# Layer 1's weight conversions with one step on ScalarE, splits in halves, and a new order at the front and in layer 2

## The chip, the core and the metric

One NeuronCore of a Trainium2 chip runs the whole program in one launch. Five engines work from queues of their own, each in order: TensorE (matmuls, and the weight loads that go beside them), VectorE (DVE in the rows), ScalarE (ACT), GpSimd (POOL) and SyncE (SP, which here issues every DMA). They wait for one another by semaphores. The metric is the time of one execution on the device in microseconds, the median of three runs.

## The reference

Three layers follow one another on 4 batches of 576 tokens, 2304 in all, 512 values each.

- Attention by landmarks, 8 heads of 64: `A = softmax(q k_lm)`, `Bm = softmax(q_lm k_lm)`, `C = softmax(q_lm k)`, where `q_lm` and `k_lm` are means over 18 tokens (32 landmarks). `Z` is an approximate inverse of `Bm` after six steps `Z = 2 Z - Z Bm Z`. The result is `A Z C v`.
- Layer 1: `h = x w_in` (512 to 2048), `g = h * clip(h + 3, 0, 6) / 6`, then `g w_out` (2048 to 512).
- Layer 2: the same shapes with `g = P(h) / (Q(h) + 1e-6)`, `P` a cubic with coefficients `a`, `Q = 1 + |b0| |h| + |b1| h^2`.

The four weight matrices arrive in 64-bit floating point, and the chip works in 32 bits. The inputs are drawn at a large scale, so that single-pass matmuls would not be precise enough.

## The kernel before, in words

*Precision.* Each large matmul is done as three: both factors are split into a high half (a copy to the type fp32r) and a low half (the value less the high one), and high x high, high x low and low x high are summed in PSUM. `split` (L95 to L104) writes the high half on one engine (mostly ScalarE, L99) and the low one on another (mostly GpSimd, L104).

*Weights.* Each matrix comes in 8 pieces of 1024 values on each of 128 partitions, 32 pieces in all, listed in `convs`: the first 16 are layer 1's (`wi` from `w_in`, `w1` from `w_out`), the others layer 2's. A piece is loaded by `cv_load` as raw 64-bit words, two DMAs of 512 KB, the first four into slabs, the later ones into a pool of two buffers. `cv_bits` (L134 to L148) makes 32-bit values of it: ScalarE scales the high word's absolute value into the exponent range (L145), VectorE shifts that left by three (L146), ors in the top three bits of the low word (L147) and ors in the sign (L148). The first four pieces go through it in halves, which gives 8 times 512 values, the other 28 whole. A `w1` or layer 2 piece is then split by `cv_split`; layer 2's halves are written to DRAM and come back when layer 2 begins. A `wi` piece is not split: it is stored, and loaded again for batches 1 to 3.

*The front of layer 1.* `w_in` is folded into attention: for each batch `T` (from `tmat`, a 64 x 32 matrix for each head) is multiplied with `w_in`, which gives `U` (`u_visit`, matmuls in L232, high half by ScalarE L495, low half by VectorE L496). Each quarter of `U` needs two `wi` pieces and serves four chunks. `AT` is the transposed `A`, made in two halves of a batch (`scores_a`, `soft_a1` to `soft_a3`).

*Chunks.* Layer 1 runs over 128 chunks: 8 blocks of 288 tokens by 16 chunks of 128 of the 2048 inner values. Blocks 0 and 1 take turns after 8 chunks, so that the later weights are wanted later. A chunk is `l1_in` (6 matmuls `psh`, L520; Relu on ScalarE, L523; `g` on VectorE, L525), `l1_split`, and four chunks later `l1_out` (12 matmuls into the four `psy` banks, L543). After a block's last chunk its `y` is evicted (L567 to L571) and stored.

*What sets the order.* Each step of attention, conversion and chunk is given a place by `at(place, f, ...)`; one unit is one chunk. The steps are emitted in the order of places, and a planner then orders the instructions of each engine by that priority and by a simulated timeline, in which an instruction that is ready may go ahead. The places are numbers in the table `PRM`: `f` and `a0`, `a1` for batch 0's attention, `cv` for conversions, `bt` for the attention of later batches, `u0`, `ul`, `uh` for batch 0's visits of `U`. Warm-up matmuls (`warm`) fill TensorE at the start.

*PSUM.* A pool `ps_l1` holds four banks shared by small results and `psh` (tag `psx`), and the four `psy` banks. When layer 1 is done, `ps_l2` is laid over them: four `ph` banks first, then `po`.

*Layer 2.* 48 units (6 blocks of 384 tokens by 8 pairs of inner chunks) in an order written out by hand: in turn n the matmuls `ph` of unit n (L730), its polynomial (`l2_poly`: ScalarE L740 and L741, `q` on GpSimd L742 and L743, or on VectorE in units listed in `FAST`), the split of unit n-1, the logarithm and exponential that stand for a division (L754, L755), the products on VectorE (L760 to L764), and the matmuls `po` of unit n-2 (L783). The units in `FAST` are worked in halves.

Of the kernel before, what the change touches and what calls it, by code (L numbers as in the profile page):

```python
# [36 lines left out]


PRM = dict(
    a0=[-53.53, -50.35, -44.44, -37.85],  # L40
    a1=[-28.73, -13.04, -13.56, -1.27],
    u0=-5.4,
    ul=2.4,
    uh=-0.88,
    nsl=4,
    f=[-78.2, -63.24, -60.85, -62.05, -59.74, -59.16, -58.38, -57.2, -56.3, -55.43, -55.23, -53.49, -53.31, -53.27, -52.82, -50.61, -43.53, -46.73, -41.98],
    fin=1.11,
    cv=[-62.23, -38.38, -34.15, -32.98, -29.24, -27.11, -6.27, -3.82, 6.49, 9.04, 10.58, 11.59, 12.99, 13.4, 14.91, 19.54],
    w0=32.18,
    ws=6.32,  # L50
    bt=[
# [11 lines left out]
def fused(ctx: ExitStack, tc: tile.TileContext, qT, kT, v, w_in, w_out, w2_in, w2_out, ca, cb, out):  # L63
# [26 lines left out]
    QC = 1.0 + 1e-6  # L90
    G.memset(lnb[:, 0:1], QC * 2.0 ** -LNS)
    G.memset(lnb[:, 1:2], -LNS * math.log(2.0))
    ca_s = const.tile([P, 4], F32, name="ca_s")
    cb_s = const.tile([P, 2], F32, name="cb_s")

    def split(dst_hi, dst_lo, src, hi_eng, lo_eng):

        if hi_eng is A:
            A.activation(dst_hi, src, AF.Copy)  # L99
        elif hi_eng is G:  # L100
            G.tensor_scalar(dst_hi, src, 1.0, 0.0, op0=ALU.mult, op1=ALU.add)
        else:
            V.tensor_copy(dst_hi, src)
        lo_eng.tensor_tensor(dst_lo, src, dst_hi.bitcast(F32), op=ALU.subtract)  # L104
# [26 lines left out]
            for h, t in enumerate(raw[key]):  # L131
                SP.dma_start(t.rearrange("p (a b) -> p a b", a=a // 2), src[:, h * a // 2:(h + 1) * a // 2])

    def cv_bits(key, h):  # L134
        if h == 0:
            val[key] = slab.tile([P, GW], F32, tag="slab", name="val")
        parts = raw[key]
        if h >= len(parts):
            return
        n = GW // len(parts)  # L140
        t = val[key][:, h * n:(h + 1) * n]
        i = t.bitcast(U32)
        w = parts[h].bitcast(U32).rearrange("p (n two) -> p n two", two=2)
        lo, hi = w[:, :, 0], w[:, :, 1]
        A.activation(t, hi.bitcast(F32), AF.Abs, scale=2.0 ** -112)  # L145
        V.tensor_scalar(i, i, 3, None, op0=ALU.logical_shift_left)  # L146
        V.scalar_tensor_tensor(i, in0=lo, scalar=29, in1=i, op0=ALU.logical_shift_right, op1=ALU.bitwise_or)  # L147
        V.scalar_tensor_tensor(i, in0=hi, scalar=0x80000000, in1=i, op0=ALU.bitwise_and, op1=ALU.bitwise_or)  # L148

    def cv_split(key):  # L150
        src = val.pop(key)
        hi = slab.tile([P, GW], F32R, tag="slab", name="whi")
        lo = slab.tile([P, GW], F32R, tag="slab", name="wlo")
        split(hi, lo, src, A, G)
# [41 lines left out]
    st = {}  # L196

    def psa(tag="psa"):
        return pp.tile([P, 512], F32, tag="psx" if tag in ("psa", "psh") else tag, name=tag, bufs=4 if tag in ("psa", "psh") else 1)

    def load_kq(b, cut=1):
        kx[b] = att.tile([P, NPAIR, S + LM], F32, tag="kx", name="kx")
# [323 lines left out]
    def l1_split(n):  # L528
        gg = hps.pop(n)
        t = w1p.tile([P, 2, HB], F32R, tag="ghl", name="ghl", bufs=5)  # L530
        split(t[:, 0, :], t[:, 1, :], gg, A, G)
        ghl[n] = t

    def l1_out(n):
        blk, c = turn[n]
        c0, c1 = (0, NFC - 1) if blk > 1 else (c - c % HC, c - c % HC + HC - 1)
        if c == c0:
            yps[blk] = [pp.tile([P, 512], F32, tag=f"psy{e}", name="psy") for e in range(NDC)]
        ps, t = yps[blk], ghl.pop(n)
# [76 lines left out]
    def at(place, f, *a):  # L616
        plan.append((place, len(plan), f, a))
# [39 lines left out]
        ):  # L657
            at(t, w, 0, h)
    for u in range(NG // 2):
        j = 2 * u  # L660
        at(PRM["u0"] if u == 0 else (2 * j if j < 4 else 2 * j + 8 - PRM["uh"]) - PRM["ul"], u_visit, 0, (u,))
    at(-100, warm, PRM["wm"][0], lambda: ident)
    at(f0[4] + 1e-3, warm, PRM["wm"][1], lambda: st[0, "qs"].rearrange("p a m -> p (a m)"))
    at(f0[6] + 1e-3, warm, PRM["wm"][2], lambda: st[0, "bd"][:, 0, 0].rearrange("p a m -> p (a m)"))
# [4 lines left out]
        cvp.append(PRM["cv"][i] if i < 2 * NG else PRM["w0"] + PRM["ws"] * (i - 2 * NG))  # L669
    for i in range(len(convs)):  # L670
        for h in range(2):
            at(cvp[i] + 0.1 * h, cv_bits, convs[i], h)
        at(cvp[i] + max(PRM["fin"], 0.2), cv3, convs[i])
        at(-99.5 + 0.1 * i if i < 4 else -98 + 0.01 * i if i < NSL else min(cvp[i - 2] + 0.9, cvp[i] - 0.1), cv0, i)

# [31 lines left out]
    l2_load = L2P["load"]  # L707
    pw1.__exit__(None, None, None)
    ps_l1.__exit__(None, None, None)


    l2p = L2P["p"]
# [84 lines left out]
                SP.dma_start(out[j * T2 + m * P:j * T2 + (m + 1) * P, :], o)  # L797

    NN = NB2 * NU2
    FAST = (0, 1, NN - 2, NN - 1)  # L800
    ms = tc.manual_schedule()
    ms.__enter__()
    for n in range(NN + 2):
        if n == 0:
            for j in range(NG):
                w2_load("i", j, (L2P["p"] if j == 0 else slab, slab))
                w2_load("o", j, (slab, slab))
        j, u = divmod(n, NU2)
# [75 lines left out]
```

## Time and profile before

| | us |
|---|---|
| median of 3 runs | 851.72 (850.27 to 851.88) |
| the profiled execution | 851.85 |
| its span, first to last instruction | 850.1 |
| TensorE busy | 818.7 (96%) |
| VectorE busy | 576.8 (68%) |
| ScalarE busy | 473.4 (56%) |
| GpSimd busy | 486.9 (57%) |
| mean granted clock of TensorE | 0.98 |

A busy share is a mean over stages. TensorE counts as busy while a matmul is under way, also at the lower clock and also for the warm-up matmuls, so its 96% say little of the front. The rows further down are of views that cut the execution by stage, by what an engine waited for, by kind of instruction and by order of time.

### The profile page before, as it was taken

What the parts mean: (1) busy time and instruction counts of PE and PEld (TensorE: products, weight loads), DVE (VectorE), ACT (ScalarE), POOL (GpSimd) and SP (SyncE); (2) the same over time, 40 slices, a digit from 0 to 9 for tenths busy, and PEclk for the clock granted to TensorE, in tenths of its full rate; (3) what the DMA queues carried; (4) which work ended last, traced back from release to release, by engine and by line L of the source; (5) the groups of instructions that cost most, each with busy time, mean ns of one, the idle gap of its engine ahead of it and who ended that gap; (6) DMA issues with size and microseconds to landing.
All of it is one profiled execution on the core that took longest, in us unless ns stands there. A gap on an engine that the chain in (4) does not pass through costs nothing.

```text
span 850.1 us, 14978 instructions
## 1 busy us (share of the span) xinstructions
PE 818.7 (96%) x5778; PEld 743.3 (87%) x5778; DVE 576.8 (68%) x935; ACT 473.4 (56%) x864; POOL 486.9 (57%) x353
## 2 busy tenths in 40 slices
PE   9769989999998999899999999999999999999998
PEld 8638879989898898889998889898989989898986
DVE  6989988695776646674228776665766675766666
ACT  3445665564564536655436656566656666565654
POOL 1249455553576325977315975766774775675551
PEclk9858999999999999999999999999999999999999
DMA  9765487393669205886891011011010010100101
GB/s 352 288 239 170 162 298 283 98 339 124 239 215 324 86 29 182 267 282 244 317 349 55 0 38 38 1 38 38 0 38 32 7 38 1 37 1 1 38 1 37
DMA packets 46312, 113.17 MB, mean 133 GB/s; under 512 B 6177, under 2 KB 14369, under 8 KB 45857
## 3 DMA queue, kind: packets, MB, share of 16 engines
q1 hardware_dynamic: 46240, 112.22, 37.6%
q8 instruction: 45, 0.74, 0.4%
q14 instruction: 27, 0.21, 0.1%
HBM read 81.79 MB, written 30.41 MB: 132 GB/s over the span
## 4 chain that ended last, share of the span: by engine, by line
PE 61%; DVE 15%; DMA 9%; ACT 5%; POOL 4%; issue 4%; SPq 0%; DVEq 0%; ACTq 0%; POOLq 0%
PE po L783 21%; PE ph L730 20%; PE psy L543 12%; PE psh L520 5%; DMA raw<-in_moe_w_in 3%; DMA qx<-in_q 3%; DVE val L148 3%; DVE val L147 2%; DMA yd<-y 2%; PE psa L232 1%; ACT val L145 1%; DVE val L146 1%; DVE g L525 1%; POOL ghl L104 1%; DMA wis<-wid 1%
## 5 line engine op out<-in xcount | busy, mean ns | idle before, releaser
L543 PE MATMUL psy<-ghl,whi 128*128 128x288 f32 x1024 | 217.8, 300 | 9.6 <-POOL ghl L104 5.2
L783 PE MATMUL po<-w2s,g2hl 128*128 128x512 f32 x864 | 210.4, 396 | 1.5 <-POOL g2hl L104 1.5
L730 PE MATMUL ph<-yhl,w2s 128*128 128x384 f32 x1152 | 208.5, 336 | 0.6 <-DVE y L571 0.6
L730 PEld LDWEIGHTS ph<-yhl,w2s 128*128 128x128 f32 x1152 | 202.1, 188 | 5.0 <-DVE y L571 0.8
L104 POOL TENSOR_TENSOR ghl<-g,ghl 128x288 fp32r<-128x288 f32 x128 | 135.0, 1064 | 120.2 <-ACT ghl L99 113.2
L783 PEld LDWEIGHTS po<-w2s,g2hl 128*128 128x128 f32 x864 | 161.8, 188 | 37.8 <-POOL g2hl L104 2.8
L543 PEld LDWEIGHTS psy<-ghl,whi 128*128 128x128 f32 x1024 | 167.7, 190 | 20.2 <-POOL ghl L104 6.7
L543 PE MATMUL psy<-ghl,wlo 128*128 128x288 f32 x512 | 149.1, 298 | 0.0
L520 PE MATMUL psh<-AT,us 128*128 128x288 f32 x768 | 127.8, 305 | 7.0 <-ACT us L495 3.4
L760 DVE SCALAR_TENSOR_TENSOR q<-q,r 128x768 f32<-128x768 f32 (+1 forms) x52 | 46.6, 895 | 114.7 <-ACT r L755 114.7
L520 PEld LDWEIGHTS psh<-AT,us 128*128 128x128 f32 x768 | 111.5, 194 | 11.1 <-ACT us L495 4.2
L742 POOL TENSOR_SCALAR q<-t,cb_s 128x768 f32<-128x768 f32 x44 | 56.0, 1272 | 102.1 <-ACT t L740 102.1
L104 POOL TENSOR_TENSOR g2hl<-g,g2hl 128x768 fp32r<-128x768 f32 (+1 forms) x52 | 89.8, 1729 | 34.1 <-ACT g2hl L99 34.1
L543 PEld LDWEIGHTS psy<-ghl,wlo 128*128 128x128 f32 x512 | 96.4, 189 | 1.2 <-issue 1.2
L525 DVE SCALAR_TENSOR_TENSOR g<-r,psh 128x288 f32<-128x288 f32 x128 | 56.8, 448 | 59.5 <-ACT r L523 42.7
L99 ACT ACTIVATE ghl<-g 128x288 fp32r<-128x288 f32 x128 | 55.7, 441 | 69.3 <-DVE g L525 62.5
L754 ACT ACTIVATE r<-q,lnb 128x768 f32<-128x768 f32 (+1 forms) x52 | 46.3, 890 | 81.4 <-POOL q L743 75.9
L743 POOL TENSOR_TENSOR q<-q,t 128x768 f32<-128x768 f32 x44 | 84.5, 1920 | 3.7
L523 ACT ACTIVATE r<-psh,three 128x288 f32<-128x288 f32 x128 | 62.7, 496 | 40.9 <-PE psh L520 40.9
L104 POOL TENSOR_TENSOR wlo<-val,whi 128x1024 fp32r<-128x1024 f32 x24 | 59.1, 2463 | 43.8 <-ACT whi L99 40.2
L740 ACT ACTIVATE t<-ph 128x384 f32<-128x384 f32 x96 | 47.0, 490 | 57.7 <-PE ph L730 57.3
L761 DVE SCALAR_TENSOR_TENSOR p<-p,ca_s,r 128x768 f32<-128x768 f32 (+1 forms) x52 | 64.6, 1243 | 0.0
(140 smaller groups left out, 995.2 us busy)
## 6 DMA issues: line engine op xcount, KB each, us to landing
raw<-in_moe_w_in SPq DMA_DIRECT2D x32, 512.0 KB, 5.7
raw<-in_moe_w_out SPq DMA_DIRECT2D x32, 512.0 KB, 5.7
wis<-wid SPq DMA_DIRECT2D x24, 512.0 KB, 7.1
w2s<-w2di SPq DMA_DIRECT2D x16, 512.0 KB, 6.2
w2s<-w2do SPq DMA_DIRECT2D x16, 512.0 KB, 5.8
yd<-y SPq DMA_DIRECT2D x32, 144.0 KB, 4.0
out<-o SPq DMA_DIRECT2D x18, 256.0 KB, 2.1
vx<-in_v SPq DMA_DIRECT2D x4, 1024.0 KB, 7.7
```

Of the source, the lines that this page charges most:

```text
L99: A.activation(dst_hi, src, AF.Copy)
L104: lo_eng.tensor_tensor(dst_lo, src, dst_hi.bitcast(F32), op=ALU.subtract)
L520: PE.matmul(ps[:, :HB], u[:, wp, f0:f0 + P], at[:, xp, g, :], start=(k == 0), stop=(k == 5))
L523: A.activation(r, ps[:, :HB], AF.Relu, bias=three)
L525: V.scalar_tensor_tensor(gg, in0=r, scalar=6.0, in1=ps[:, :HB], op0=ALU.min, op1=ALU.mult)
L543: PE.matmul(ps[e][:, :HB], w1[c // 2][wp][:, o + e * P:o + (e + 1) * P], t[:, xp, :], start=(c == c0 and i == 0), stop=(c == c1 and i == 2),)
L730: PE.matmul(ps[i][:, :T2], w2i[u][wp][:, d * 256 + i * P:d * 256 + (i + 1) * P], yh[:, xp, d, :], start=(k == 0), stop=(k == 11),)
L740: A.activation(t[:, i], h, AF.Abs)
L742: eng.tensor_scalar(q[:, cs], t[:, cs], cb_s[:, 1:2], cb_s[:, 0:1], op0=ALU.mult, op1=ALU.add)
L743: eng.tensor_tensor(q[:, cs], q[:, cs], t[:, cs], op=ALU.mult)
L761: V.scalar_tensor_tensor(p, in0=p, scalar=ca_s[:, 0:1], in1=r, op0=ALU.add, op1=ALU.mult)
L783: PE.matmul(ops[j][m], t[:, xp, i, m * P:(m + 1) * P], w2o[u][wp][:, i * DM:(i + 1) * DM], start=(c == 0 and k == 0), stop=(c == NFC - 1 a ...
```

## The change

`cv_bits` gets a flag. For all 16 pieces of layer 1 (`ka` lists 0 to 15) the shift by three is no instruction of its own: ScalarE reads the low word's top byte, divides it by 32, rounds down with a bias and writes the result as a 32-bit integer over the low word; VectorE then shifts and ors in one instruction. The bias is found at the start by two small instructions (`probe`) that tell how the conversion to an integer rounds. `cv_split` works in halves of 512, in both layers. In chunks from 96 on the low half of `g` is subtracted by VectorE instead of GpSimd. The `psx` banks get a pool of their own, opened ahead of `ps_l1`. In layer 2 unit 1 leaves `FAST`, and `q` is VectorE's in unit 0 only. Batch 0's four visits of `U` have places of their own (`ub`), and nearly all other places get new numbers.

```diff
-    a0=[-53.53, -50.35, -44.44, -37.85],
-    a1=[-28.73, -13.04, -13.56, -1.27],
-    u0=-5.4,
-    ul=2.4,
-    uh=-0.88,
+    a0=[-53.44, -49.77, -45.07, -40.67],
+    a1=[-29.09, -5.95, -16.01, -2.05],
+    ub=[-11.56, 2.59, 9.82, 14.37],
+    hc=8,
-    fin=1.11,
+    fin=0.75,
-    cv=[-62.23, -38.38, -34.15, -32.98, -29.24, -27.11, -6.27, -3.82, 6.49, 9.04, 10.58, 11.59, 12.99, 13.4, 14.91, 19.54],
-    w0=32.18,
+    cv=[-62.22, -38.38, -34.15, -33.16, -30.24, -27.99, -7.31, -4.94, 5.33, 7.88, 9.53, 12.36, 12.49, 13.12, 14.89, 21.57],
+    w0=31.92,
...
+    probe = const.tile([P, 3], F32, name="probe")
+    G.memset(probe[:, 0:1], 0.75)
+    A.activation(probe[:, 1:2].bitcast(I32), probe[:, 0:1], AF.Copy)
+    A.activation(probe[:, 2:3], probe[:, 1:2].bitcast(I32), AF.Copy, scale=-31.0 / 64.0)
+    floor_b = probe[:, 2:3]
...
         A.activation(t, hi.bitcast(F32), AF.Abs, scale=2.0 ** -112)
-        V.tensor_scalar(i, i, 3, None, op0=ALU.logical_shift_left)
-        V.scalar_tensor_tensor(i, in0=lo, scalar=29, in1=i, op0=ALU.logical_shift_right, op1=ALU.bitwise_or)
+        if by_act:
+            b = parts[h].bitcast(U8).rearrange("p (n k) -> p n k", k=8)[:, :, 3]
+            A.activation(lo.bitcast(I32), b, AF.Identity, bias=floor_b, scale=1.0 / 32.0)
+            V.scalar_tensor_tensor(i, in0=i, scalar=3, in1=lo, op0=ALU.logical_shift_left, op1=ALU.bitwise_or)
+        else:
+            V.tensor_scalar(i, i, 3, None, op0=ALU.logical_shift_left)
+            V.scalar_tensor_tensor(i, in0=lo, scalar=29, in1=i, op0=ALU.logical_shift_right, op1=ALU.bitwise_or)
         V.scalar_tensor_tensor(i, in0=hi, scalar=0x80000000, in1=i, op0=ALU.bitwise_and, op1=ALU.bitwise_or)
...
-        split(hi, lo, src, A, G)
+        for h in range(2):
+            c = slice(h * HW, (h + 1) * HW)
+            split(hi[:, c], lo[:, c], src[:, c], A, G)
...
+    ps_x = tc.tile_pool(name="ps_x", bufs=4, space=PSUM)
+    px = ps_x.__enter__()
...
-        split(t[:, 0, :], t[:, 1, :], gg, A, G)
+        split(t[:, 0, :], t[:, 1, :], gg, A, V if n >= 6 * NFC else G)
...
-        j = 2 * u
-        at(PRM["u0"] if u == 0 else (2 * j if j < 4 else 2 * j + 8 - PRM["uh"]) - PRM["ul"], u_visit, 0, (u,))
+        at(max(f0[-1] + 1e-4, PRM["ub"][u]), u_visit, 0, (u,))
...
-    FAST = (0, 1, NN - 2, NN - 1)
+    FAST = (0, NN - 2, NN - 1)
...
-            l2_poly(n, i, V if n in FAST else G)
+            l2_poly(n, i, V if n == 0 else G)
```

## Rows read from the trace of the kernel before

**Rows 1.** Busy time by stage: PE, PEld, DVE, ACT, POOL, then PE clock, DMA share, GB/s.
```profile
53.70:70.40 16.70, 14.91 (x81) 11.74 (x82) 15.89 (x21) 8.81 (x16) 12.28 (x8) 0.55 0.54 203
70.40:173.70 103.30, 98.31 (x977) 88.55 (x981) 87.06 (x158) 60.77 (x128) 60.95 (x47) 1.00 0.60 204
173.70:368.00 194.30, 187.78 (x1780) 174.06 (x1781) 131.38 (x257) 106.93 (x232) 104.90 (x85) 0.99 0.58 200
368.00:440.10 72.10, 70.47 (x528) 70.01 (x527) 25.77 (x41) 32.32 (x66) 37.63 (x34) 1.00 0.84 303
440.10:846.30 406.20, 404.17 (x2016) 363.21 (x2016) 275.35 (x371) 242.82 (x380) 257.37 (x160) 1.00 0.08 26
```

**Rows 2.** Timeline of TensorE, first chunks: start, duration, engine, line, operation [idle before].
```profile
53.71 2.77 PE L520 MATMUL psh<-AT,us 128*128 128x288 f32 x10 [3.35 <-ACT us L495]
...
70.15 0.29 PE L543 MATMUL psy<-ghl,wlo 128*128 128x288 f32 x1
```

**Rows 3.** Waits of TensorE, whole span: us in total, times, longest.
```profile
PE psy L543 <- POOL ghl L104: 5.2, 5, 2.1
PE psh L520 <- ACT us L495: 3.4, 1, 3.4
...
PE psh L520 <- DVE us L496: 2.7, 3, 1.8
PE psy L543 <- ACT y L569: 2.2, 1, 2.2
```

**Rows 4.** L146 alone by stage: length, VectorE busy (instructions), clock, DMA share, GB/s.
```profile
0.00:53.70 53.70, 6.23 (x11) 0.85 0.85 312
53.70:70.40 16.70, 2.96 (x2) 0.55 0.54 203
70.40:150.00 79.60, 6.01 (x7) 1.00 0.65 227
```

**Rows 5.** Groups by line and shape: busy us, mean ns of one, idle before.
```profile
L145 ACT ACTIVATE val<-raw 128x1024 f32<-128x1024 f32 x28 | 32.0, 1141 | 6.7 <-DMA raw<-in_moe_w_out 4.2 <-DMA raw<-in_moe_w_in 2.5
...
L145 ACT ACTIVATE val<-raw 128x512 f32<-128x512 f32 x8 | 5.5, 686 | 12.5 <-DMA raw<-in_moe_w_in 10.9 <-DMA raw<-in_moe_w_out 1.6
...
L104 POOL TENSOR_TENSOR ghl<-g,ghl 128x288 fp32r<-128x288 f32 x128 | 135.0, 1064 | 120.2 <-ACT ghl L99 113.2 <-PE psy L543 4.9 <-POOL ghl L104 0.7
...
L104 POOL TENSOR_TENSOR wlo<-val,whi 128x1024 fp32r<-128x1024 f32 x24 | 59.1, 2463 | 43.8 <-ACT whi L99 40.2 <-PE psh L520 2.9 <-ACT ev L465 0.7
```

**Rows 6.** Chain that ended last, 25 to 55 us: start, us, what.
```profile
30.55 0.10 DVE val L146
...
38.90 0.69 DVE val L146
...
45.66 0.68 DVE val L146
```

**Rows 7.** Timelines of ScalarE and VectorE around U's first visit.
```profile
52.49 0.68 ACT L257 ACTIVATE sT<-sT 128x576 f32<-128x576 f32 x1 [4.74 <-POOL sT L256]
53.08 1.07 ACT L495 ACTIVATE us<-psa 128x512 fp32r<-128x512 f32 x2
...
56.18 1.91 DVE L146 TENSOR_SCALAR val<-val 128x1024 uint32<-128x1024 uint32 x1 [0.77 <-ACT val L145]
```

**Rows 8.** Timelines of TensorE and GpSimd at the start of layer 2.
```profile
440.63 12.77 PE L730 MATMUL ph<-yhl,w2s 128*128 128x384 f32 x72 [0.55 <-DVE y L571]
453.24 4.37 PE L783 MATMUL po<-w2s,g2hl 128*128 128x512 f32 x18
...
463.30 4.01 PE L783 MATMUL po<-w2s,g2hl 128*128 128x512 f32 x16 [1.03 <-POOL g2hl L104]
...
451.17 1.02 POOL L104 TENSOR_TENSOR g2hl<-g,g2hl 128x384 fp32r<-128x384 f32 x1 [16.57 <-ACT g2hl L99]
...
458.41 1.76 POOL L742 TENSOR_SCALAR q<-t,cb_s 128x768 f32<-128x768 f32 x1 [3.95 <-ACT t L740]
460.26 2.03 POOL L743 TENSOR_TENSOR q<-q,t 128x768 f32<-128x768 f32 x1
```

**Rows 9.** What SP's queue waited for, whole span: us in total, times, longest.
```profile
SPq L128 <- DVE val L148: 126.5, 23, 13.4
```

More of the change, by code (lines that the diff above doesn't have):

```diff
@@ L13 @@
 I64 = mybir.dt.int64
+I32 = mybir.dt.int32
+U8 = mybir.dt.uint8
 AF = mybir.ActivationFunctionType
@@ L39 @@
 PRM = dict(
-    a0=[-53.53, -50.35, -44.44, -37.85],
-    a1=[-28.73, -13.04, -13.56, -1.27],
-    u0=-5.4,
-    ul=2.4,
-    uh=-0.88,
+    a0=[-53.44, -49.77, -45.07, -40.67],
+    a1=[-29.09, -5.95, -16.01, -2.05],
+    ub=[-11.56, 2.59, 9.82, 14.37],
+    hc=8,
     nsl=4,
-    f=[-78.2, -63.24, -60.85, -62.05, -59.74, -59.16, -58.38, -57.2, -56.3, -55.43, -55.23, -53.49, -53.31, -53.27, -52.82, -50.61, -43.53, -46.73, -41.98],
-    fin=1.11,
-    cv=[-62.23, -38.38, -34.15, -32.98, -29.24, -27.11, -6.27, -3.82, 6.49, 9.04, 10.58, 11.59, 12.99, 13.4, 14.91, 19.54],
-    w0=32.18,
+    f=[-78.2, -63.94, -61.56, -62.67, -60.44, -59.97, -59.25, -58.2, -57.19, -56.63, -58.76, -55.22, -52.89, -55.22, -53.55, -51.43, -44.54, -49.77, -31.24],
+    fin=0.75,
+    cv=[-62.22, -38.38, -34.15, -33.16, -30.24, -27.99, -7.31, -4.94, 5.33, 7.88, 9.53, 12.36, 12.49, 13.12, 14.89, 21.57],
+    w0=31.92,
     ws=6.32,
     bt=[
[3 rows of a table removed]
[3 rows of a table added]
     ],
     lp=[1, 1, 0, 0],
+    ka=[0, 1, 2, 3, 4, 5, 6, 7, 8, 9, 10, 11, 12, 13, 14, 15],
     wm=[45, 25, 15],
@@ L132, in cv_load, with cv_bits @@
                 SP.dma_start(t.rearrange("p (a b) -> p a b", a=a // 2), src[:, h * a // 2:(h + 1) * a // 2])
-    def cv_bits(key, h):
+    def cv_bits(key, h, by_act):
         if h == 0:
@@ L198, in psa @@
     def psa(tag="psa"):
-        return pp.tile([P, 512], F32, tag="psx" if tag in ("psa", "psh") else tag, name=tag, bufs=4 if tag in ("psa", "psh") else 1)
+        if tag in ("psa", "psh"):
+            return px.tile([P, 512], F32, tag="psx", name=tag)
+        return pp.tile([P, 512], F32, tag=tag, name=tag)
     def load_kq(b, cut=1):
@@ L501, in fused @@
     hps, ghl, yps = {}, {}, {}
-    HC = NFC // 2
-    turn = [(blk, c) for p in range(2) for blk in range(2) for c in range(p * HC, (p + 1) * HC)]
+    HC = PRM["hc"]
+    turn = [(blk, c) for p in ((0, HC), (HC, NFC)) for blk in range(2) for c in range(*p)]
     turn += [(blk, c) for blk in range(2, 2 * B) for c in range(NFC)]
@@ L535, in l1_out @@
         blk, c = turn[n]
-        c0, c1 = (0, NFC - 1) if blk > 1 else (c - c % HC, c - c % HC + HC - 1)
+        c0, c1 = (0, NFC - 1) if blk > 1 else (0, HC - 1) if c < HC else (HC, NFC - 1)
         if c == c0:
@@ L671, in fused @@
         for h in range(2):
-            at(cvp[i] + 0.1 * h, cv_bits, convs[i], h)
+            at(cvp[i] + 0.1 * h, cv_bits, convs[i], h, i in PRM["ka"])
         at(cvp[i] + max(PRM["fin"], 0.2), cv3, convs[i])
@@ L709, in fused @@
     ps_l1.__exit__(None, None, None)
+    ps_x.__exit__(None, None, None)
     l2p = L2P["p"]
```

6 rows, old and new, of the table bt are left out of this document.

## The prediction

> **What bounds the kernel now.** The profiled execution took 851.85 us, 850.1 of them between the first and the last instruction; the median of the three runs is 851.72, so a sum made against this execution stands for the median within 0.02%. What this kernel's measurement can tell from no change is about 0.2%, some 1.7 us.
>
> The first view to read is the table by stage [rows 1]. From 440.1 to 846.3 TensorE is busy 404.17 of 406.2 us: layer 2 is its own matmuls, and nothing beside TensorE's queue can make it shorter by more than 2 us. From 70.4 to 440.1 the three rows between leave 4.99, 6.52 and 1.63 us open, 13.1 together. So the place with room is the first 70.4 us, at whose end the twelfth psy matmul finishes the first chunk of layer 1 [rows 2]. The stretch from 53.7 to 70.4 is the telling one: VectorE is busy 15.89 of 16.7 us, ScalarE 8.81, and TensorE, busy 14.91, works at a granted clock of 0.55, close to the lower of its levels (1.2 of 2.4 GHz), after a stage in which it had stood still between small matmuls. Second comes the list of what TensorE waited for [rows 3]. The longest single wait is 3.4 us for the eviction of U (ScalarE, L495); 5.2 us in five pieces are for the low half that GpSimd subtracts (L104), 2.7 us for U's low half on VectorE, 2.2 us for an eviction of y (L569).
>
> **The change part by part.**
>
> *The shift (A).* All 16 conversions of layer 1 lose one VectorE instruction, L146, and gain one ScalarE instruction that reads a byte at a step of 8 and writes 32 bits at a step of 8. What goes, by time [rows 4]: 6.23 us before 53.7, 2.96 up to 70.4, 6.01 up to 150, together 15.2 us in 20 instructions (8 halves, 12 whole ones). What comes: no row shows such an instruction; the nearest is L145, which reads four bytes at the same step: 686 ns for 512 elements, 1141 for 1024 [rows 5]. Eight and twelve of them make 5.5 + 13.7 = 19.2 us of ScalarE. If the narrow read or the stepped write ran at half that pace it would be 38 us; below L145's time I see no reason to go. I take 19.2. The added wait: the first logical VectorE instruction of a conversion now waits for two ScalarE instructions, and behind the second one there stand in ScalarE's queue the evictions of U, the Relus and the high halves.
>
> Before 53.7 the chain of waits carries 0.10 + 0.69 + 0.68 = 1.5 us of L146 between the landmark matrix and T [rows 6]: that comes off the path, within 0 and the 6.23 us that VectorE loses there. I take 1.5. From 53.7 to 70.4 VectorE has under 1 us of slack and 2.96 us go, while ScalarE has 7.9 us open and gets two instructions, 2.3 us; I take 2.0, within 3.0 and a loss of 2.3 (both new ones ahead of a Relu). From 70.4 to 150 seven go, 6.01 us, but TensorE loses only about 5 us in that whole stage [rows 1], so I take 1.0, within a loss of 4.0 (half of seven ScalarE instructions ahead of TensorE's needs) and a gain of 3.
>
> A rule of the Trainium skill speaks against this part. The page "ScalarE: Activation LUTs", section "Rules for kernel authors", says to give adding, maximum, multiplying and the like to VectorE, not to ScalarE. By it a whole conversion would be 1.14 - 0.68 = 0.46 us longer. The trace agrees on the single instruction (0.68 us on VectorE at 45.66, 1.14 on ScalarE [rows 5, 6]), but not on the engine with room, and the same L146 took 1.91 us at 56.18 [rows 7].
>
> *U of batch 0 in four places (B).* The first visit's matmuls end 3.35 us before the chunks' first at 53.71 [rows 2], at 50.36, but ScalarE evicts from 53.08 on: ahead in its queue stands the exponential of the second half's softmax, 4.74 us late because of GpSimd's subtraction [rows 7]. The new places put this visit (-11.56) ahead of that softmax step (-5.95); before it was -5.4 behind -13.04. If the planner follows, the eviction starts after the matmuls: 53.08 - 50.36 = 2.7 us. The bounds are 0 and the whole wait of 3.4. What is late next is AT's second half, not needed before the chunks of block 1. The visits for U's third and fourth quarter move 4.7 and 4.1 places forward, and past them their 32 small matmuls each, with the evictions and the low halves on ScalarE and VectorE. Of TensorE's waits for U's low half one of 1.8 is in the stage counted under A, and 0.9 us is left in two; on the other side a visit placed early waits for its second weight slab in TensorE's queue, as long as one conversion. I cost it at nothing, with 1 us either way.
>
> *Splits in halves.* 24 weight splits become two ScalarE and two GpSimd instructions each. From L145's two sizes, 2 x 686 - 1141 = 0.23 us more each on ScalarE, 5.5 us in all; and on GpSimd I take as much [rows 5]. What hides it: both engines are idle four tenths of the time from 70.4 to 368 [rows 1]. What it gives: the first half of wlo is there a microsecond earlier, and a chunk's low half stands behind some 1.2 us of GpSimd work and not 2.46. Of the 5.2 us of waits for GpSimd I take 0.5, within -2 and 3.
>
> *Last 32 chunks: low half on VectorE.* 32 x 1.06 us leave GpSimd [rows 5]; VectorE gets 32 subtractions that no row shows at this size; they cost it nothing at best and GpSimd's 34 us at worst. From 368 to 440.1 VectorE is busy only 25.77 of 72.1 us, which covers even that. TensorE has 1.63 us open there, so no more can be won [rows 1]. I take 0, within 1.6 and a loss of 2. The Trainium skill bears on it: "SBUF — State Buffer", section "SBUF: two separate sides", has VectorE and GpSimd share a port pair as an exclusive lock, which an instruction with two SBUF inputs also needs. By it each of these subtractions could wait out half of a GpSimd split, 1.2 us; the trace agrees that VectorE's times stretch so (the 1.91 us above), and with it the stage would still be covered.
>
> *Layer 2's start, the PSUM pool (C).* The first matmul of layer 2 waits 0.55 us for a bank of y [rows 8]. With chunk banks in a pool of their own, the new pool's first four banks are those, free since the last Relu: -0.55. Unit 1 no longer goes in halves on VectorE; its q goes whole to GpSimd, 1.76 + 2.03 us as unit 2's does [rows 8], ahead of unit 0's low half (1.02). Unit 1's matmuls, the second 24 of the 72, end near 448.5; with the step on ScalarE the low half is there near 453.9, and the third po matmul, wanted near 453.2 (0.55 earlier than now), waits 0.6 to 1.2; I take 0.9. In return unit 1 is through before its po is due at 461, and the 1.03 us before 463.30 goes. Together 0.55 + 1.03 - 0.9 = 0.7, within 1.6 and a loss of 0.6 (nothing goes, the wait is full).
>
> *The end and the rest.* Units 46 and 47 give q to GpSimd; which relieves VectorE. Of the 2.03 us that layer 2 leaves open [rows 1] 0.45 remain beside the two waits above; I take them off, and at worst they double. All other places move, with their DMAs on SP's queue (two of 512 KB for each conversion, the stores, the y). The wait for y, 2.2 us [rows 3], stays, within 3 us either way. The probe's instructions run at the start, where ScalarE waits for its first data.
>
> Sum: 1.5 + 2.0 + 1.0 + 2.7 + 0.5 + 0.7 + 0.45 = 8.85 us; 851.85 - 8.85 = 843.0, and 842.9 from the median: 843. Its own range is 837.5 to 848: the terms' bounds are wide, but they are unlikely to fall on one side.
>
> **The rivals.**
>
> *The gain is given back.* The loads of raw weights have two buffers, and SP waited 126.5 us in 23 pieces for the last VectorE instruction of a conversion [rows 9]. If conversions, not TensorE, pace the chunks up to 174, an earlier start only waits longer there. Then the terms before 150 and U's 2.7 go, and 0.5 + 0.7 + 0.45 stay: 850.2. For it: those waits. Against it: TensorE was busy 98.31 of 103.3 us there.
>
> *The clock comes early.* If the filled front lets TensorE work from 53.7 at the upper level, its 14.91 us of work at 0.55 would be 8.2: another 6.7 us, 836. For it: the clock stands at 1.00 from 70.4 on, where TensorE is never idle for long. Against it: the stage before has its holes still.
>
> *Slower: ScalarE's queue.* The new instructions stand in order ahead of evictions and Relus. If all of A is lost and half of the twelve whole ones lies on TensorE's path, that is 12 x 0.57 = 6.8 us against 2.7 + 0.7 + 0.45 kept: 854.8. It decides from 3.85 / 12 = 0.32 us each, 28% of one. For it: ScalarE already made TensorE wait 3.4 us in this way. Against it: it is idle nearly half of the stage. The ScalarE rule named above is this rival's.
>
> *The planner does not do it.* The places are wishes; if U's first visit is still behind the exponential, 2.7 us stay: 845.7, within the forecast's own range.
>
> **How the numbers follow.** The forecast with the planner's case 0.50, given back 0.19, clock 0.17, slower 0.14. Faster than 850.0: 0.50 + 0.17 + half of the second, 0.77. Within 0.2%: the other half and a little of the last, 0.12. Slower: 0.11. From 834 to 853 the range leaves out a part of the clock case below and most of the slower one above.
>
> **What would show it.** A: VectorE in the 16.7 us before the first finished chunk no longer full, the new ScalarE rows near 0.69 and 1.14 us, T's copy 1 to 3 us earlier. B: no wait of TensorE for L495 above 1 us. C: no idle time before the first ph, one wait of under 1 us at the first po. The first finished chunk should be 5 to 7 us before 70.4, and layer 2 should start as much earlier and about 2 more. Wrong would be: new rows above 2 us, or an earlier first chunk with the end of layer 1 near 440.

## The result, and the profile after

| | before | after |
|---|---|---|
| median, us | 851.75 (850.27 to 851.88, 4 runs) | 840.5 (840.03 to 842.21, 4 runs) |
| ratio of the times, 95% interval | 1 | 0.9875 [0.9858, 0.9893] |
| profiled execution, its span | 851.85, 850.1 | 842.21, 840.4 |

The change makes the kernel 11.2 us faster; the forecast was 843, with a range of its own from 837.5 to 848. The profiled execution of after is the slowest of its four, so the traces have 9.6 us to explain.

By stage, as in [rows 1] (stage and its length, busy time of TensorE, its weight loads, VectorE, ScalarE and GpSimd with counts, TensorE's granted clock, DMA share, GB/s):

```profile
45.40:62.10 16.70, 12.72 (x121) 8.17 (x121) 11.96 (x19) 13.56 (x21) 9.31 (x8) 0.79 0.68 244
53.70:70.40 16.70, 13.24 (x98) 11.37 (x91) 13.46 (x18) 10.41 (x19) 14.96 (x11) 0.90 0.51 174
...
70.40:173.70 103.30, 94.13 (x899) 83.26 (x899) 73.66 (x145) 64.91 (x131) 53.93 (x49) 0.95 0.55 194
173.70:368.00 194.30, 192.53 (x1849) 180.54 (x1848) 135.29 (x271) 113.37 (x253) 104.01 (x95) 1.00 0.59 206
368.00:432.90 64.90, 64.86 (x488) 64.63 (x487) 34.94 (x64) 29.30 (x65) 9.26 (x8) 1.00 0.91 327
432.90:836.70 403.80, 402.64 (x2018) 361.96 (x2016) 270.76 (x356) 242.17 (x377) 268.62 (x169) 1.00 0.08 27
```

The same 16.7 us of the front now run at 0.90 of the clock, not 0.55. From 70.4 to 173.7 TensorE has 9.17 us open, where it had 4.99, and 0.95 of the clock, not 1.00. From 173.7 to 368 it has 1.77 open, where it had 6.52, and after 368 nothing. So the front got better, the stage behind it worse, and the quiet stage after that, of which little had been expected, better again.

TensorE's timeline of the front (start, duration, engine, line, operation, count, idle before it), to be read against [rows 2]; L542 is the old L520, L566 the old L543:

```profile
50.10 2.85 PE L542 MATMUL psh<-AT,us 128*128 128x288 f32 x18 [0.76 <-ACT us L517]
...
60.78 0.40 PE L566 MATMUL psy<-ghl,whi 128*128 128x288 f32 x1 [1.66 <-POOL ghl L112]
...
61.94 0.69 PE L566 MATMUL psy<-ghl,whi 128*128 128x288 f32 x4
```

The chunks start 3.6 us earlier than at 53.71, and the wait for U is 0.76 us, not 3.35. The first chunk is finished at 62.1, in the last row's four matmuls, 8.3 us earlier.

The waits of TensorE, as in [rows 3], and under them one of SP's queue, as in [rows 9] (us in total, times, longest):

```profile
PE psy L566 <- POOL ghl L112: 4.7, 5, 1.8
PE psa L418 <- ACT e L373: 3.7, 1, 3.7
...
PE po L806 <- POOL g2hl L112: 1.1, 1, 1.1
PE psy L566 <- ACT y L592: 1.1, 1, 1.1
PE psh L542 <- ACT us L517: 0.8, 1, 0.8
```
```profile
SPq L136 <- DVE val L162: 92.4, 19, 10.7
```

The wait of 3.7 us is new, and now the longest. It begins at 89.98; the timelines of TensorE, ScalarE and VectorE there:

```profile
93.69 1.12 PE L418 MATMUL psa<-ident,e 128*128 128x128 f32 x4 [3.71 <-ACT e L373]
```
```profile
89.23 1.14 ACT L153 ACTIVATE val<-raw 128x1024 f32<-128x1024 f32 x1
90.25 1.28 ACT L157 ACTIVATE raw<-raw,probe 128x1024 int32<-128x1024 uint8 x1
91.44 0.67 ACT L279 ACTIVATE sT<-sT 128x576 f32<-128x576 f32 x1
92.01 0.86 ACT L545 ACTIVATE r<-psh,three 128x288 f32<-128x288 f32 x2
92.78 0.76 ACT L373 ACTIVATE e<-e,cnb 128x576 f32<-128x576 f32 x1
```
```profile
90.28 1.22 DVE L162 SCALAR_TENSOR_TENSOR val<-raw,val 128x1024 uint32<-128x1024 uint32 x1
91.41 0.16 DVE L364 TENSOR_SCALAR cnb<-cmx 128x2 f32<-128x2 f32 x1
```

An exponential of batch 1 (L373), which TensorE needs, stands in ScalarE's queue behind a conversion's two instructions, the new one (L157) among them. But the queue is the smaller part of the wait. The exponential also reads `cnb`, a negated maximum, and VectorE has that written only at 91.57, because a conversion's instruction (L162) stands ahead of it in VectorE's order. L157 is through at 91.53, just before. So 1.6 us of the wait pass before the exponential could have started, 1.2 us go to what ScalarE does first then (another exponential, L279, and two Relus, L545, all behind L157), and 0.9 us to the exponential itself. The mechanism of the rival on ScalarE's queue is there, and it is worth at most 1.2 us directly.

**The ledger.** Up to the first matmul of layer 2 TensorE runs the same 3762 matmuls in every kernel here. So the moment at which layer 2 starts is the sum of two things that can be added up from TensorE's timeline: the gaps between matmuls, and the busy time, which for the same matmuls differs by their pace, the clock above all. Gaps by stage, in us of each profiled execution:

```
                       gaps 0-70  70-175  175-layer 2   busy   layer 2 starts   median
before                   12.4       5.0       8.7       414.5      440.6        851.75
after                    11.1       9.1       1.8       410.9      432.9        840.5
after, once more (e5)    10.8       8.1       2.4       410.0      431.1        841.8
e1 no byte               11.6       7.2       2.6       413.2      434.5        845.0
e2 old front             13.8       7.5       2.0       415.0      438.3        848.9
e8 U's old place         15.0       5.4       3.8       410.6      434.6        842.4
e6 batch 1 old places    11.3      10.2       3.4       409.5      434.4        843.8
e7 two pieces back       10.3       5.8       3.1       413.5      432.9        841.2
e4 six slabs             10.2      11.6       1.8       417.3      440.9        850.3
e12 splits whole         10.7       9.2       5.6       410.4      435.9        845.5
e3 low half on GpSimd    10.7       8.1       3.5       411.0      433.3        843.5
e9 y free                 9.6       6.6       4.3       413.4      433.9        844.5
e10 before, y free       13.1       5.7       9.1       414.0      441.9        854.0
e11 old layer 2          10.1       7.5       1.9       412.4      431.8        841.5
```

Layer 2 starts 7.7 us earlier: 3.6 from the pace, 1.3 from gaps of the front, 6.9 from gaps after 175, less 4.1 that gaps from 70 to 175 take back. The rows of after and e5 are of one and the same kernel: they differ by up to 1.0 us in a column and 1.8 us in the start of layer 2, so that smaller differences between rows say little. Layer 2 itself gives 1.9 more (405.7 to 403.8 us).

### The profile page after: what moved, and what is told of

Its sections match the earlier page's. It is cut to its first block, busy times and chain, and to the rows that moved or that the text cites. A ratio compares the mean times of both kernels' runs of the same rounds, so it can differ in the third digit from the quotient of the medians.

```text
span 840.4 us, 15001 instructions
## 1 busy us (share of the span) xinstructions
PE 813.5 (97%) x5778; PEld 739.4 (88%) x5778; DVE 566.5 (67%) x932; ACT 492.5 (59%) x907; POOL 465.9 (55%) x355
## 4 chain that ended last, share of the span: by engine, by line
PE 75%; DMA 8%; DVE 5%; ACT 4%; POOL 4%; issue 3%; SPq 0%; ACTq 0%; DVEq 0%; POOLq 0%
PE po L806 24%; PE ph L753 23%; PE psy L566 16%; PE psh L542 7%; DMA raw<-in_moe_w_out 3%; PE psa L254 2%; DMA raw<-in_moe_w_in 2%; DMA qx<-in_q 2%; DMA yd<-y 1%; ACT val L153 1%; POOL ghl L112 1%; POOL wlo L112 1%; DVE val L162 1%; PE psa L480 1%; DMA yr<-yd 1%
## 5 line engine op out<-in xcount | busy, mean ns | idle before, releaser
L566 PE MATMUL psy<-ghl,whi 128*128 128x288 f32 x1024 | 216.5, 301 | 7.9 <-POOL ghl L112 4.7
L566 PEld LDWEIGHTS psy<-ghl,whi 128*128 128x128 f32 x1024 | 166.0, 189 | 18.2 <-POOL ghl L112 7.2
L112 POOL TENSOR_TENSOR ghl<-g,ghl 128x288 fp32r<-128x288 f32 x96 | 96.4, 1013 | 99.7 <-ACT ghl L107 84.0
L566 PE MATMUL psy<-ghl,wlo 128*128 128x288 f32 x512 | 147.7, 295 | 0.0
L765 POOL TENSOR_SCALAR q<-t,cb_s 128x768 f32<-128x768 f32 (+1 forms) x49 | 60.3, 1231 | 154.6 <-ACT t L763 154.6
L783 DVE SCALAR_TENSOR_TENSOR q<-q,r 128x768 f32<-128x768 f32 (+1 forms) x51 | 48.4, 949 | 117.5 <-ACT r L778 117.1
L542 PE MATMUL psh<-AT,us 128*128 128x288 f32 x768 | 124.4, 301 | 2.1 <-DVE us L518 1.4
L542 PEld LDWEIGHTS psh<-AT,us 128*128 128x128 f32 x768 | 108.5, 190 | 6.4 <-DVE us L518 2.4
L112 POOL TENSOR_TENSOR wlo<-val,whi 128x512 fp32r<-128x512 f32 x48 | 64.8, 1372 | 68.7 <-ACT whi L107 67.9
L566 PEld LDWEIGHTS psy<-ghl,wlo 128*128 128x128 f32 x512 | 96.2, 188 | 0.0
L766 POOL TENSOR_TENSOR q<-q,t 128x768 f32<-128x768 f32 (+1 forms) x49 | 91.6, 1869 | 4.1
L545 ACT ACTIVATE r<-psh,three 128x288 f32<-128x288 f32 x128 | 62.5, 496 | 34.7 <-PE psh L542 34.7
```

The lines of the kernel that those rows point to most:

```text
L542: PE.matmul(ps[:, :HB], u[:, wp, f0:f0 + P], at[:, xp, g, :], start=(k == 0), stop=(k == 5))
L545: A.activation(r, ps[:, :HB], AF.Relu, bias=three)
L566: PE.matmul(ps[e][:, :HB], w1[c // 2][wp][:, o + e * P:o + (e + 1) * P], t[:, xp, :], start=(c == c0 and i == 0), stop=(c == c1 and i == 2),)
L765: eng.tensor_scalar(q[:, cs], t[:, cs], cb_s[:, 1:2], cb_s[:, 0:1], op0=ALU.mult, op1=ALU.add)
L766: eng.tensor_tensor(q[:, cs], q[:, cs], t[:, cs], op=ALU.mult)
L783: V.scalar_tensor_tensor(q, in0=q, scalar=QC, in1=r, op0=ALU.add, op1=ALU.mult)
```

## The experiments

Twelve kernels, each an edit of the changed kernel unless it says otherwise. The planner orders the work anew for each, so an edit also moves steps further on. The kernel before ran beside them, with medians of 851.93 (e1 to e4), 851.33 (e5 to e8) and 851.7 (e9 to e12).

**e5, the changed kernel once more.** 841.81 us (837.95 to 846.83, 6 runs), ratio 0.9887 [0.9856, 0.9918]. Its runs spread over 9 us, so a difference of under 2 us between two kernels below says nothing by its median.

> The kernel after once more, unchanged, so that the others of this set have it beside them. Both theories: 839.5 to 841.5. In its profile TensorE again waits 3 to 4 us near 90 us for an exponential of batch 1 (L373) that stands in ScalarE's queue, if that wait belongs to the order of the queue and not to one execution.

The new wait is there again, 3.74 us: it is no accident of one execution.

**e1, the shift back on VectorE.**
```diff
-    ka=[0, 1, 2, 3, 4, 5, 6, 7, 8, 9, 10, 11, 12, 13, 14, 15],
+    ka=[],
```


> The kernel after, but all of layer 1's conversions shift on VectorE again (L146's instruction back, no byte read on ScalarE). Theory 'given back': from chunk 8 on the chunks wait for conversions, whose pace is set by the two raw buffers and not by VectorE, so the end moves by 1.5 us at most: 840 to 842. Theory 'front', the prediction's: the shift is worth 4.5 us before 150, so 845.

844.99 us, ratio 0.9922 [0.9898, 0.9947]. The new instruction is worth 3.2 to 4.5 us, against the two medians of after: what the prediction's part A had, 4.5. But it does not arise as that part had it. T's copy starts at 50.13, 2.9 us later than in after, and the first chunk ends at 68.0, not 62.1: 5.9 us, where 3.5 had been forecast to there. Layer 2 then starts only 1.6 us later (3.4 against e5). Busy time is 2.3 us more. TensorE waits for the exponential of batch 1 here too, 1.7 us.

**e2, the front's places as before** (the softmax steps, Newton steps, conversions and U of batch 0).
```diff
-    a1=[-29.09, -5.95, -16.01, -2.05],
-    ub=[-11.56, 2.59, 9.82, 14.37],
+    a1=[-28.73, -13.04, -13.56, -1.27],
+    ub=[-5.4, 1.6, 14.48, 18.48],
...
```


> The kernel after, with the old places of the front (a0, a1, f, fin, cv and the old places of batch 0's U). Theory 'given back': the first chunk ends 4 to 8 us later, near 66 to 70, chunk 28 within 2 us of the kernel after (which ends it at 165.8), and the end stays at 840 to 842.5. Theory 'front': the 8 us at the first chunk reach the end, 846 to 848.

848.92 us, ratio 0.9973 [0.9951, 0.9994]: 7 to 8 us of the change's 11 depend on these places. The stage of its front, as in [rows 1]:

```profile
53.70:70.40 16.70, 13.81 (x84) 10.28 (x84) 14.56 (x18) 9.76 (x16) 11.92 (x9) 0.61 0.50 172
```

With the new instruction but the old places the clock is 0.61, close to the 0.55 of before. By the ledger 4.1 us of pace and 2.7 of gaps in the front separate it from after.

**e8, U's first visit alone in its old place** (and the softmax steps around it).
```diff
-    a1=[-29.09, -5.95, -16.01, -2.05],
-    ub=[-11.56, 2.59, 9.82, 14.37],
+    a1=[-29.09, -13.04, -13.56, -2.05],
+    ub=[-5.4, 2.59, 9.82, 14.37],
```


> The kernel after, with the first visit of batch 0's U at its old place behind the second half's softmax (-5.4, behind -13.04 and -13.56). The prediction priced this at 2.7 us. If the price holds to the end: first chunk's matmuls start 2.5 to 3.5 us after 50.1, and the end is 842.5 to 844. If the front's gain is given back at the waits between 85 and 160: the end is 839.5 to 841.5.

842.37 us, ratio 0.9891 [0.9869, 0.9913], not to be told from after. The wait for U is 5.3 us, the chunks start 2.7 us later (52.8), and the first one ends at 68.0. Yet layer 2 starts only 1.7 us later: what the front lost, the gaps from 70 to 175 (5.4, not 9.1) gave back, and what is left is mostly a wait for y near 277, of 3.0 us and not 1.1. The gain of an early U is real where it arises and mostly gone further on.

**e4, six weight slabs ahead.** The theory: conversions, held by two raw buffers, set the pace up to 174.
```diff
-    nsl=4,
+    nsl=6,
```


> The kernel after, with the first 6 instead of 4 raw pieces loaded into slabs, so that the two raw buffers begin at piece 6. Theory 'given back': the last conversion of layer 1 ends 4 us or more before 127.1, chunks 12 to 28 come 3 us or more earlier, and the end is 834 to 838. Theory 'front': the buffers set nothing, 839.5 to 841.5.

850.25 us, ratio 0.9978 [0.9965, 0.9992]. The last conversion ends at 111.3, not 127.1, and the kernel is 8 to 10 us slower: gaps from 70 to 175 are 11.6, busy time 417.3. The theory's forecast fell. The edit slowed the front as well (the first chunk ends at 68.2, not 62.1, at a granted clock of 0.65 from 50 to 70), and it holds raw pieces in slabs that the weights use too, so it does not test the two buffers alone. That the earlier conversions take ScalarE, VectorE and GpSimd away from the chunks is a guess; it is not shown.

**e7, conversions 11 and 12 with the shift on VectorE; e6, batch 1's places as before.** Both were to take away the 3.7 us wait.
```diff
-    ka=[0, 1, 2, 3, 4, 5, 6, 7, 8, 9, 10, 11, 12, 13, 14, 15],
+    ka=[0, 1, 2, 3, 4, 5, 6, 7, 8, 9, 10, 13, 14, 15],
```


> The kernel after, with the shift of pieces 11 and 12 alone back on VectorE: they are the two whose byte reads stand ahead of the exponential that TensorE waits for near 90. Theory 'ScalarE's queue': the 3.7 us wait there falls by 1 to 2.5 us and the end is 838 to 839.5. Theory 'early attention': the wait is set by VectorE's maximum and the order of places, and VectorE gets 1.4 us more there; the end is 840 to 842.

```diff
-        [4.17, 4.18, 8.48, 5.72, 8.92, 8.94, 9.9, 5.56, 11.67, 8.28, ...],
+        [4.17, 4.18, 7.67, 8.17, 8.67, 9.17, 9.67, 10.17, 11.67, 11.56, ...],
```


> The kernel after, with batch 1's old places (first row of bt), which let its attention come later. Theory 'early attention': the new places of batch 1 bring the transposes to TensorE's queue ahead of ScalarE's exponential; with the old ones the 3.7 us wait near 90 goes and chunk 28 ends 3 us or more before 165.8; the end is 836 to 839. Theory 'ScalarE's queue': wherever the transposes stand, the exponentials stand behind the new byte reads; the wait only moves, and the end stays at 839.5 to 842.

841.16 us, ratio 0.9869 [0.9841, 0.9897], and 843.82, ratio 0.9909 [0.989, 0.9929]. The wait is gone in both, and others stand in its place: in e7 one of 3.0 us at 90.6 for a high half, in e6 1.7 and 2.1 us from 84 to 88 and 2.9 at 119. The waits move; neither edit gains. In e7 the gaps from 70 to 175 do fall, to 5.8, but busy time rises by 2.6. And e7 speaks for VectorE near 90, as its theory "early attention" had it: with the two byte reads gone ScalarE stands idle there, waiting for VectorE's `g`, and the exponential comes no earlier (93.83), for VectorE writes its `cnb` at 93.5. ScalarE's timeline of e7:

```profile
93.12 0.81 ACT L107 ACTIVATE ghl<-g 128x288 fp32r<-128x288 f32 x2 [2.68 <-DVE g L547]
```

**e12, each weight split whole.**
```diff
-        for h in range(2):
-            c = slice(h * HW, (h + 1) * HW)
-            split(hi[:, c], lo[:, c], src[:, c], A, G)
+        split(hi, lo, src, A, G)
```


> The changed kernel with each weight split whole: one ScalarE and one GpSimd instruction. Prediction's step: the halves give 0.5 us in waits for GpSimd's low half; 841.5 to 842. Rival 'the halves are what shortened the chunks after 64' (a chunk's low half stands behind 1.2 us of GpSimd work, not 2.46): the waits for GpSimd between 280 and 370 come back, 2.1 and 1.8 us as in the kernel before, and the time is 844 to 845. Rival 'they only add instructions': 840 or less.

845.52 us, ratio 0.9938 [0.9921, 0.9956]: 3.7 to 5 us longer, not 0.5. The size is that of the first rival, its mechanism is not: between 175 and 430 TensorE waits 0.8 us for GpSimd's low half, but 4.4 for y. The longest, in TensorE's timeline:

```profile
410.30 0.54 PE L564 MATMUL psy<-ghl,whi 128*128 128x288 f32 x2 [2.50 <-ACT y L590]
```

Gaps after 175 are 5.6 us, not 1.8. They are not those of before: of the two waits that the rival names, before has 2.1 us for GpSimd at 356.0 and 1.6 us, for y, at 371.5, and neither is in e12. Why whole splits put this block's y later against its stores, the runs do not show; the order of the late chunks is another.

**e3, the last 32 chunks' low half on GpSimd again.**
```diff
-        split(t[:, 0, :], t[:, 1, :], gg, A, V if n >= 6 * NFC else G)
+        split(t[:, 0, :], t[:, 1, :], gg, A, G)
```


> The kernel after, with the low half of the last 32 chunks on GpSimd again. The trace shows the kernel after gaining 4.8 us on the one before between chunks 92 and 100. Theory 'given back': that is this edit, so 844 to 846. Theory 'front', the prediction's: the edit is worth nothing, 840 to 841.

843.5 us, ratio 0.9901 [0.9876, 0.9925]; by the median 1.7 to 3 us, just short of what can be told. The trace says 1.7 (gaps after 175 of 3.5; 1.1 against e5), and it is the wait that the edit was costed on (between 175 and 430; us in total, times, longest), 0.4 us in after and in e5:

```profile
PE psy L566 <- POOL ghl L112: 2.4, 4, 1.1
```

**e9 and e10, two y of block 3 in a tile of their own.** From the first eight kernels I took the wait for y near 272 for a place that swallows what arrives early: before lost 2.2 us there and needed 14.7 us from chunk 64 to 68; after lost 1.06 us, at 274.8, and needs 9.0. e9 edits the changed kernel, e10 the kernel before.
```diff
+                elif blk == 3 and e >= 2:
+                    if e == 2:
+                        ys = slab.tile([P, GW], F32, tag="slab", name="ys")
+                    y = ys[:, (e - 2) * HW:(e - 2) * HW + HB]
```


> Block 3's third and fourth y go to a tile of the slab pool instead of the two y buffers, so they need not wait until the stores of the first two have landed. [...] Theory 'the wait for y takes up what arrives earlier': the wait goes, the stretch from the end of chunk 64 to the end of chunk 68, 9.0 us, becomes 7.5 to 8, and the end comes 1 to 2 us earlier, 839.5 to 840.5. Rival 'there is no slack ahead to use': chunk 68 ends earlier, but the next wait (a low half from GpSimd, or a weight slab, since one slab tile is taken) gives it back by chunk 100, and the time stays at 841 within 1.

> The same edit in the kernel before, where TensorE waited 2.2 us for y at 271.5 and the clock then fell to 0.64; its chunks 64 to 68 took 14.7 us, against 9.0 in the changed kernel. Theory 'the wait for y and the clock behind it are the 5 us that the change won there': this edit alone takes 4 to 5 us off those chunks, 848 at the end, and about half of the change's gain is a wait that another edit could have had. Rival 'the 2.2 us alone': 2 us off, 849.7. Rival 'given back': chunk 68 ends earlier and chunk 100 where it did, 851.5.

844.51 us, ratio 0.992 [0.9905, 0.9935], and 853.99, ratio 1.0029 [1.0016, 1.0042]. The wait is gone and chunks 64 to 68 take 8.4 us in e9 (7.5 to 8 expected) and 10.3 in e10, as the theory said, and both kernels are slower. A few microseconds on, in TensorE's timelines of e9 and of e10:

```profile
286.48 0.66 PE L418 MATMUL psa<-ident,e 128*128 128x128 f32 x4 [2.58 <-ACT e L373]
```
```profile
288.66 1.12 PE L396 MATMUL psa<-ident,e 128*128 128x128 f32 x4 [2.41 <-ACT e L351]
```

The matmuls of the chunks were done sooner, but the exponential of a later batch that is wanted next came hardly sooner, or later: it starts at 285.6 in e9 and at 286.0 in after, at 287.7 in e10 and at 285.3 in before. So TensorE waited for it. The theory fell, and with it a way of reading: the number of a chunk is no measure of how far the kernel is, while attention work can stand ahead of it or behind. Between the ends of chunks 64 and 68 TensorE runs 48 other matmuls in before, 40 in e10, and 8 in after and e9. The ledger counts them all.

**e11, layer 2's start and end as before.**
```diff
-    FAST = (0, NN - 2, NN - 1)
+    FAST = (0, 1, NN - 2, NN - 1)
-            l2_poly(n, i, V if n == 0 else G)
+            l2_poly(n, i, V if n in FAST else G)
...
```


> The changed kernel with the old start and end of layer 2: units 1, 46 and 47 in halves on VectorE, one PSUM pool for all banks. Theory (the prediction's step, with the sizes that the changed trace showed): layer 2's first matmul waits 0.55 us again, the one before the third group of output matmuls 1.0, and the 1.15 us wait for GpSimd goes; 1 to 1.5 us longer than the changed kernel, 842 to 843. Rival 'only the PSUM pool matters': 0.5 us. Rival 'layer 2's own pace differs': the waits are as in the kernel before, but the layer is 404 us, not 405.7, and the time stays within 0.5.

841.47 us, ratio 0.9889 [0.9862, 0.9917], within 1 us of after by the median. The trace has the sizes; TensorE's timeline of e11:

```profile
431.82 12.77 PE L748 MATMUL ph<-yhl,w2s 128*128 128x384 f32 x72 [0.55 <-DVE y L590]
...
454.47 4.00 PE L801 MATMUL po<-w2s,g2hl 128*128 128x512 f32 x16 [1.03 <-POOL g2hl L112]
```

Both old waits are back, and layer 2 takes 404.8 us, 1.0 more than in after.

No kernel here is faster than the changed one by more than its runs spread. What e1, e2, e12 and e3 lose adds up to 16 to 21 us, more than the change's 11: the parts overlap, and their prices can't be added.

## Why the prediction held, and where it did not

*The shift before 53.7: 1.5 forecast, 0.8 measured with the new places.* T's copy starts at 47.25, not 48.06. That is not the shift alone: without the new instruction the new places have it at 50.13 (e1), with the instruction the old ones at 48.61 (e2). Among the new places the shift is worth 2.9 us here. The chain of waits of after shows why (start, us, what), beside [rows 6]:

```profile
30.39 1.05 ACT val L153
31.44 1.23 ACT raw L157
...
32.70 1.24 DVE val L158
```

The new instruction stands on the chain where L146 was. Its price was forecast as that of L145; the groups by line and shape (busy us, mean ns) have 768 and 1253 ns, a tenth more than 686 and 1141:

```profile
L157 ACT ACTIVATE raw<-raw,probe 128x1024 int32<-128x1024 uint8 x12 | 15.0, 1253 | 2.2 <-DMA raw<-in_moe_w_in 1.8 <-DMA raw<-in_moe_w_out 0.4
...
L157 ACT ACTIVATE raw<-raw,probe 128x512 int32<-128x512 uint8 x8 | 6.1, 768 | 0.0
```

*U's first visit: 2.7 forecast, 2.6 less wait at its place.* ScalarE's timeline has the planner's answer: the eviction (L517) goes ahead of the exponential (L279), in [rows 7] it was behind.

```profile
49.45 1.09 ACT L517 ACTIVATE us<-psa 128x512 fp32r<-128x512 f32 x2 [1.83 <-PE psa L254]
50.42 1.15 ACT L153 ACTIVATE val<-raw 128x1024 f32<-128x1024 f32 x1
51.45 0.70 ACT L279 ACTIVATE sT<-sT 128x576 f32<-128x576 f32 x1
```

At the end it is worth less, 0.6 us by the median beside it and 1.7 by layer 2's start (e8).

*The shift from 53.7 to 70.4: 2.0 forecast.* Of the 8.3 us that the first chunk came earlier 3.6 are before it, so 4.7 arise here. VectorE is no longer full (11.96 of 16.7 us), as the step said, and the clock is higher. From the chunks' first matmul to the end of the first chunk after needs 12.0 us and e1 14.4, so the shift is worth 2.4 among the new places. How the rest divides is not shown: e11, e12 and e3 have a clock of 0.74 to 0.80 from 50 to 70, not 0.91, and end the first chunk within 0.9 us of after. The rival "the clock comes early" came partly true: it had 6.7 us more, and the ledger shows 3.6 less busy time, after the dips further on.

*The shift from 70.4 to 150: a gain of 1.0 forecast, a loss found.* This is the step that failed. Without the new instruction (e1) the first chunk ends 5.9 us later than in after, but layer 2 starts only 1.6 us later; against e5 it is 6.6 and 3.4. So 3.2 to 4.3 us of what the shift gains in the front are lost behind it, where 1.0 was to be added. Gaps from 70 to 175 went from 5.0 to 9.1 us, and the clock to 0.95. The loss is not the new instruction's alone: e8, which has it, delays the first chunk by the same 5.9 us and layer 2 by 1.7, with gaps of 5.4 there, and e1, which has it not, has gaps of 7.2. In both most of an earlier front is lost behind it; of e2's 8.0 us at the first chunk 5.4 are left at layer 2. So two rivals were partly right, though not by their prices. "The gain is given back" was to be the raw buffers' doing, which no run here shows, e4 being no clean test. The queue is 1.2 us of the 3.7 us wait, and VectorE's late maximum 1.6; the queue was to cost more than the new instruction gains, but without the instruction the kernel is slower (e1). The rule of the Trainium skill, page "ScalarE: Activation LUTs", section "Rules for kernel authors", would have such arithmetic on VectorE; the 845.0 us of e1 against 840.5 and 841.8 speak against it here, the 1.2 us in the queue for it. The root of the loss in this stage stays open.

*The halves: 0.5 forecast, 3.7 to 5 lost without them (e12). The low half on VectorE: 0 forecast, 1.1 to 1.7 by the trace (e3).* These two terms were mis-sized. The gaps after 175 that [rows 1] shows, 6.52 and 1.63, were taken as nearly fixed; 6.9 of 8.7 us went, and they went also with the old front (e2: 2.0 left) and without the new instruction (e1: 2.6). The bound for the halves (3) was too small. The 32 subtractions took 0.55 us each on VectorE in the mean, against 1.01 for the others on GpSimd. TensorE's longest waits after 175 in before (us in total, times, longest):

```profile
PE psy L543 <- POOL ghl L104: 3.0, 3, 2.1
PE psy L543 <- ACT y L569: 2.2, 1, 2.2
PE psy L543 <- DVE y L571: 1.6, 1, 1.6
```

The longest of the first row ends at 356.0, before the last 32 chunks' low halves begin, and the third row's at 371.5. Neither comes back in e12 or e3, whose longest waits after 175 stand elsewhere: for y at 410.3 in e12, for low halves from 364 to 380 in e3. So it is not shown that the two terms together make up the 6.9 us. A rival is left untested: the new places of the later batches and of layer 2's weights (the rows of `bt`, `w0`), of which the experiments put back batch 1's alone (e6).

*The wait for y: unchanged forecast, within 3 us.* 2.2 became 1.06 in after, but 1.9 in e5, which is the same kernel. e9 and e10 show that it is not worth its length.

*Layer 2's start: 0.7 forecast, 0.4 found; its end: 0.45 forecast, 0.4 found.* TensorE's and GpSimd's timelines, against [rows 8]:

```profile
432.90 12.65 PE L753 MATMUL ph<-yhl,w2s 128*128 128x384 f32 x72
445.39 0.63 PE L806 MATMUL po<-w2s,g2hl 128*128 128x512 f32 x2
447.17 4.00 PE L806 MATMUL po<-w2s,g2hl 128*128 128x512 f32 x16 [1.15 <-POOL g2hl L112]
```
```profile
444.13 2.03 POOL L766 TENSOR_TENSOR q<-q,t 128x768 f32<-128x768 f32 x1
446.12 1.96 POOL L112 TENSOR_TENSOR g2hl<-g,g2hl 128x384 fp32r<-128x384 f32 x2
```

The 0.55 us before the first matmul is gone, the third output matmul waits 1.15 us behind unit 1's q (0.9 taken, 0.6 to 1.2 bounded), and no other wait is left: 2.03 us open became 1.16, with the 0.45 of the end gone too. The 0.55 is counted in the gaps after 175. Of the 1.9 us by which layer 2 itself is shorter 0.35 are waits, and the other 1.5 are the pace of its matmuls, which no step named. e11 gives back 0.6 of that pace, with the old units in halves; the rest no run explains.

So the total came out within 2.5 us of the median, and the list of causes only in part. The front's terms have the right sign where they arise, and are partly lost in the stage behind. That the sum fits so well is partly luck: a loss of 4.1 us in gaps from 70 to 175, where a gain of 1.0 was forecast, and 6.9 us of gaps gone after 175, where the halves had 0.5 and layer 2's first wait 0.55, nearly cancel.

## What to carry to other kernels

Cut a long kernel at a point up to which the bounding engine has the same instructions in every version, and add up its gaps and its busy time to there: a loop's counter misleads when other work can pass it. A term that is costed small because its stage is "nearly full" deserves its own bound from that stage's gaps, all of them. Before moving an instruction to an idle engine, look at what stands behind it in that engine's order at the moments when the bound engine has no other work ready. And before blaming the queue, look at when the late instruction's own inputs were there.

## What the runs showed of the hardware

- ScalarE's read of single bytes at a step of 8 with a 32-bit write at a step of 8 took 0.77 us for 512 elements and 1.25 for 1024, about a tenth above the four-byte read at that step.
- The granted clock from 50 to 70 us was 0.53 before and 0.91 in both profiles of the changed kernel, but 0.74 to 0.80 in e11, e12 and e3, where the first chunk ended at almost the same time (62.5 to 63.0, not 62.1). By stage of after, with the columns of the first table, the clock is low in the slice of the 3.7 us wait and the one behind it, and in two around a wait of 1.8 us that ends at 106.3; the second of each pair is without a gap:

```profile
90.00:95.00 5.00, 1.31 (x6) 1.28 (x7) 5.00 (x8) 4.55 (x10) 0.00 (x0) 0.84 0.43 111
95.00:100.00 5.00, 5.00 (x35) 4.96 (x34) 3.18 (x14) 4.25 (x8) 2.69 (x3) 0.82 1.00 370
...
105.00:110.00 5.00, 3.66 (x25) 2.11 (x25) 3.61 (x11) 1.13 (x3) 2.85 (x4) 0.70 0.84 292
110.00:115.00 5.00, 5.00 (x92) 4.20 (x93) 3.47 (x5) 3.25 (x5) 0.00 (x0) 0.62 0.02 5
```

- One kernel's executions spread over 8.9 us (e5); those of the kernel before beside them over 5.0 (849.87 to 854.92).
